# A decode block with its gradients on one core: the w1 gradient product of batch 0 taken from VectorE sums to TensorE pair transposes, and a second pass that starts two heads sooner

## The chip, the core and the metric

The kernel runs on one core of a Trainium2 chip. It is one launch. The metric is device time in microseconds (us), and less is better. The engines are called TensorE (PE in the profile), VectorE (DVE), ScalarE (ACT), GpSimd (POOL) and SyncE (SP). The profile is of one execution; the times are of several.

## What is computed

A pre-LayerNorm transformer block in decode (one query token, two batches), and all its gradients but those of a constant:

```python
B, D, H, Sk, Dh, Dff = 2, 640, 32, 4096, 128, 1728      # bf16 in and out
h  = x + softmax(q k^T * Dh**-0.5) v @ wo,   q = layernorm(x) @ wq     # per batch and head
h2 = h + relu(layernorm(h) @ w1) @ w2
out0 = h2
grads of (x, k_cache, v_cache, wq, wo, w1, w2) for a given grad_out    # jax.vjp
```

The two caches are 2 x 32 x 4096 x 128, that is 1 MiB for each batch, head and cache, and so are their gradients. All traffic together is 361.84 MB by the page.

## The kernel before, in words

**Two passes over the heads.** A head's tile is [128 positions, 32 chunks, 128 channels]. The first pass (`p1_iter`, one iteration `i` for each of the 64 pairs of batch and head) loads K and V of a head. It transposes K on TensorE by fp32 pairs (`pair_transpose`, L435: two bf16 columns are moved as one 32-bit word, and the copy at L440 brings the result from PSUM to SBUF), multiplies it with the query (`pair_matvec`, L448), exponentiates (L523), forms K weighted by the probabilities on VectorE (`pk`, L476), and sums on TensorE: `m_ps` (L469) and `u_ps` (L498). The second pass (`p2_iter` and `p2_tail`, one step `j` for each head) writes the gradients of K and V. For a step it needs V again (`W`), unless the tile was kept: the last six heads of a batch are kept, and they come first. It writes 2 MiB for each head (`gV` L900, `gK` L851, both from GpSimd's queue).

**The middle.** Between the passes over a batch lies `middle_gen(b)`: the sum over heads, the second LayerNorm, the MLP's hidden layer (`hf_ps`, L761), its gradient `ghfc`, then gx2 = w1 times `ghfc`, the backward LayerNorm (`gh1c`), and for each group of heads the gradient `go` with what the second pass needs (`go_group`). A head's second-pass step needs its `go_group`.

**The product gx2 = w1 times ghfc.** `spread_f` broadcasts the 14 columns of `ghfc` over the partitions (matmul L633, ScalarE copy L636) in three pieces, and 15 `ttr` instructions (L658, product and sum on VectorE) make the partial sums `gx2p`, which L794 adds up.

**The order is written out by hand.** There is a plan of iterations. `P2_AT = H + 2 + M0_ITERS` is the iteration at which the second pass joins, on every second iteration of the first. With M0_ITERS = 7 the middle of batch 0 has the iterations 34 to 40 for itself and the second pass joins at 41. From iteration 66 on there are second-pass steps alone (the tail), and batch 1's middle runs there. Background generators (the middles, `fin_gen` for the weight gradients, `gx_gen` for the gradient of x) are advanced a little after each of the eight parts of an iteration, by a credit: 0.8 for each part while a middle has the iterations for itself, 0.2 later; a bare `yield` costs 0.5. A `ttr` also waits for a `turn()`, of which an iteration in a middle gives five. If a head's `go_group` isn't issued when its step comes, `bg_until` issues all that is missing at once.

**Buffers.** 13 tiles of 1 MiB hold K, V, W and the gradients. `pump` issues loads in the order of the plan from SyncE's queue when the pool has a tile, and the load waits there for the last reader of the tile. From iteration 33 on six of the tiles are the kept V of batch 0.

Of the kernel before, what the change touches and what calls it, by code (L numbers as in the profile page):

```python
# [9 lines left out]
ALU = mybir.AluOpType  # L10
# [5 lines left out]
def kernel(  # L16
# [39 lines left out]
    NMT = (32, 12)  # L56
    NPS = 2 * H - 8

    def f_kc(c):
        return 128 if c < NFF else F_rem  # L60


# [11 lines left out]
    def pst(shape, dtype, role, name):  # L74

        k = banks[role].pop(0)
        banks[role].append(k)
        return ps.tile(shape, dtype, tag=f"bank{k}", bufs=1, name=name)
# [284 lines left out]
    NW2 = -(-NF // FP)  # L363
    w2_tiles = {}

    def load_w2(k, tag, order="(c p) d -> p c d"):

        c0, c1 = k * FP, min(NF, (k + 1) * FP)
        t = take(tag, [128, FP, D], "w2_t")
        full = min(c1, NFF)  # L370
        if full > c0:
            nc.sync.dma_start(out=t[:, 0:full - c0, :],
                              in_=B_w2[0:NFF * 128, :].rearrange(order, p=128)[:, c0:full, :])
        if c1 > NFF:
            nc.sync.dma_start(out=t[0:F_rem, NFF - c0, :], in_=B_w2[NFF * 128:Dff, :])
        return t
# [246 lines left out]
        nc.vector.tensor_tensor(out=Uc[:, b, :], in0=t[:], in1=rt[:, b, :], op=ALU.mult)  # L623


    def bcast_cols(colsrc, n, kc_of, dst, first=0):

        for c0 in range(0, n, 4):
            t = pst([128, 512], FP32, "bc", "bc_ps")
            w = 0  # L630
            for c in range(first + c0, first + min(n, c0 + 4)):
                kc = kc_of(c)
                nc.tensor.matmul(t[:, w:w + kc], lhsT=colsrc[0:kc, c:c + 1].to_broadcast([kc, 128]),  # L633
                                 rhs=ident_bf[0:kc, 0:kc], start=True, stop=True)
                w += kc
            nc.scalar.copy(out=dst[:, c0 * 128:c0 * 128 + w], in_=t[:, 0:w])  # L636
            yield

    def spread_cols(t, colsrc, n):
# [23 lines left out]
    def turn():  # L663

        while slot[0] <= 0:
            yield 0.0
        slot[0] -= 1

    def one(src, b):
        return src[:, :, b]  # L670
# [34 lines left out]
    def mlp_out():  # L705

        ml32 = fin.tile([128, ND, B], FP32, tag="ml32", bufs=1, name="ml32")
        nc.vector.memset(ml32[:], 0.0)
        while ("arow", 0) not in done:
            yield  # L710
        for k in range(NW2):
            while free["q"] < 1:
                yield
            t = load_w2(k, "q", "(p c) d -> p c d")
            yield from wait(12)
            c1 = min(NF, (k + 1) * FP)
            m_ps = pst([128, ND, B], FP32, "mid", "mlp_ps")
            for c in range(ND):
                for cf in range(k * FP, c1):
                    kc = f_kc(cf)  # L720
                    nc.tensor.matmul(m_ps[:, c, :], lhsT=t[0:kc, cf - k * FP, c * 128:(c + 1) * 128],
                                     rhs=arow[0:kc, cf, :], start=(cf == k * FP), stop=(cf == c1 - 1))
            give(t)
            yield
            nc.vector.tensor_tensor(out=ml32[:], in0=m_ps[:], in1=ml32[:], op=ALU.add)
        ml_bf = fin.tile([128, ND, B], BF16, tag="ml_bf", bufs=1, name="ml_bf")
        nc.vector.tensor_copy(out=ml_bf[:], in_=ml32[:])
        y_bf = fin.tile([128, B, ND], BF16, tag="y_bf", bufs=1, name="y_bf")
        nc.vector.tensor_tensor(out=y_bf[:].rearrange("p b c -> p c b"), in0=h1c[:], in1=ml_bf[:], op=ALU.add)
        yield from wait(3)  # L730
        for b in range(B):
            store_row(y_bf[:, b, :], ND, out_0[b].rearrange("s (c p) -> (s c) p", p=128))
            yield

    def middle_gen(b):
        if o_next[0] < (b + 1) * H // OG:
# [21 lines left out]
        for cf in range(NF):  # L758
            kc = f_kc(cf)
            for c in range(ND):  # L760
                nc.tensor.matmul(hf_ps[0:kc, cf:cf + 1], lhsT=w1_t[:, c, cf * 128:cf * 128 + kc],  # L761
                                 rhs=x2c[:, c, b:b + 1], start=(c == 0), stop=(c == ND - 1))
            yield 0.25
        nc.vector.tensor_scalar(out=acol[:, 0:NFF, b], in0=hf_ps[:, 0:NFF], scalar1=0.0, scalar2=None, op0=ALU.max)
        if F_rem:
            nc.vector.tensor_scalar(out=acol[0:F_rem, NFF, b:b + 1], in0=hf_ps[0:F_rem, NFF:NF],
                                    scalar1=0.0, scalar2=None, op0=ALU.max)
        mask = small.tile([128, NF], FP32, tag="mask", bufs=1, name="mask")
        nc.vector.tensor_single_scalar(out=mask[:], in_=acol[:, :, b], scalar=0.0, op=ALU.is_gt)
        nc.vector.tensor_tensor(out=ghfc[:, :, b], in0=ga[:, b, :], in1=mask[:], op=ALU.mult)  # L770
        yield from wait(3)
        gx2 = small.tile([128, 1, ND], FP32, tag="gx2", bufs=1, name="gx2")
        gx2p = small.tile([128, ND, 3], FP32, tag="gx2p", bufs=1, name="gx2p")

        def spread_f(k):
            r = rows3[:, 1 + k % 2, :]
            c0, c1 = k * ND, min(NF, (k + 1) * ND)
            yield from bcast_cols(one(ghfc, b), c1 - c0, f_kc, r, c0)
            rows.append((r, min(D, Dff - k * D)))

        rows = []
        yield from spread_f(0)
        for k in range(3):
            ahead = spread_f(k + 1) if k < 2 else iter(())
            r, fw_k = rows[k]
            for c in range(ND):
                yield from turn()
                ttr(w1_t[:, c, k * D:k * D + fw_k], r[:, 0:fw_k], gx2p[:, c, k:k + 1], fw_k)
                yield 0.85
                if c in (1, 3):  # L790
                    next(ahead, None)
            for _ in ahead:
                yield
        nc.vector.reduce_sum(out=gx2[:, 0, :], in_=gx2p[:], axis=AX.X)  # L794
        yield ("w1", b)
        yield from ln_bwd(gx2[:], x2c[:, :, b:b + 1], rstd2[:, b:b + 1], gc[:, :, b:b + 1], gh1c[:, :, b:b + 1], 1)
        hbc = rows3[:, 2, :]
        yield from bcast_cols(one(gh1c, b), ND, lambda c: 128, hbc)
        yield ("gh1", b)

        first = H - KEPT[b]
# [7 lines left out]
    def ga_gen():  # L809

        gbc = [rows3[:, 1 + b, :] for b in range(B)]
        for b in range(B):
            yield from bcast_cols(one(gc, b), ND, lambda c: 128, gbc[b])
        for k in range(NW2):
            while k not in w2_tiles:
                yield 0.0
            t = w2_tiles.pop(k)
            for c in range(k * FP, min(NF, (k + 1) * FP)):
                kc = f_kc(c)
                for b in range(B):  # L820
                    yield from turn()
                    ttr(t[0:kc, c - k * FP, :], gbc[b][0:kc, :], ga[0:kc, b, c:c + 1], D, kc)
                    yield 0.9
            give(t)
# [79 lines left out]

    fw = [0]

    def rows_of(pool, col, n, name, tag):

        r = pool.tile([128, n * 128], BF16, tag=tag, bufs=2 if tag == "rD" else 1, name=name)
        for c0 in range(0, n, 4):  # L910
            cn = min(4, n - c0)
            w = FIN["wide"][(c0 // 4) % 2]
            nc.scalar.copy(out=w[:, 0:cn, :, 0:B], in_=col[:, c0:c0 + cn, None, :].to_broadcast([128, cn, 4, B]))
            yield
            yield
            t = pst([128, 512], FP32, "mid", "rw_ps")
            for k in range(cn):
                nc.tensor.matmul(t[:, k * 128:(k + 1) * 128], lhsT=w[:, k, :, :].rearrange("p q x -> p (q x)"),
                                 rhs=ident_bf[:], start=True, stop=True)
            nc.scalar.copy(out=r[:, c0 * 128:(c0 + cn) * 128], in_=t[:, 0:cn * 128])  # L920
            yield 0.7
        FIN[name] = r

# [38 lines left out]
    def fin_gen(fin):  # L962
# [1 line left out]
        for w in FIN["wide"]:  # L964
            nc.vector.memset(w[:], 0.0)
        yield from wait(2)
        yield from rows_of(fin, acol, NF, "ar", "rX")
        ar_ps = pst([128, NFF, B], FP32, "mid", "ar_ps")
        for cf in range(NFF):
            nc.tensor.matmul(ar_ps[:, cf, :], lhsT=FIN["ar"][0:B, bass.ds(cf, 128, step=NFF)], rhs=ident_bf[0:B, 0:B],  # L970
                             start=True, stop=True)
        nc.scalar.copy(out=arow[:, 0:NFF, :], in_=ar_ps[:])
        if F_rem:
            nc.scalar.copy(out=arow[:, NFF, :], in_=acol[:, NFF, :])
        yield ("arow", 0)
        yield from rows_of(fin, gc, ND, "gr", "rD")
        yield from outer_rows(FIN["ar"], 0, NFF * 128, FIN["gr"], D, out_7[0:NFF * 128, :], NFF)
        if F_rem:
            yield from outer_rows(FIN["ar"], NFF * 128, F_rem, FIN["gr"], D, out_7[NFF * 128:Dff, :], 1)
        yield from rows_of(fin, ghfc, NF, "ghfr", "rX")  # L980
        yield from rows_of(fin, x2c, ND, "x2r", "rD")
        yield from outer_rows(FIN["x2r"], 0, D, FIN["ghfr"], Dff, out_6, ND)
        HH = H // 2
# [106 lines left out]
            assert bg and bg_one(bg) >= 0.0, mark  # L1090
        forced[0] = False

    M0_ITERS = 7
    P2_AT = H + 2 + M0_ITERS
    RATES = (0.2, 0.8, 0.2, 0.8, 0.45)
    RATE2 = 0.65
# [29 lines left out]
    def pump():  # L1126
        while queue:
            what, k = queue[0]
            if what == "w":
                load_weights(k)  # L1130
            else:
                tag = "ld"
                if free["ld"] < 1:
                    return
                if what == "w2":
                    w2_tiles[k] = load_w2(k, tag)
                else:
                    load_tile(what, k, tag)
            queue.pop(0)
# [142 lines left out]
```

## Time and profile before

| | |
|---|---|
| time, median of 3 runs | 897.04 us (895.9 to 898.17) |
| the profiled execution | 896.38 us, span 894.5 us |
| PE / DVE / ACT / POOL busy | 83% / 77% / 54% / 22% of the span |
| DMA over the span | 361.84 MB, 405 GB/s |
| chain that ended last | PE 40%, DMA 28%, DVE 17%, ACT 7%, issue 5% |

Busy time of PE counts the whole latency of pipelined matmuls: its pace is read from start to start. The chain's shares are averages over stages that have different limits, so the prediction reads the stage of batch 0's middle by itself.

### The profile page before, as it was taken

To read this page: it belongs to the slowest core of one execution; us is meant where nothing else is said; L and a number is where in the kernel's file an instruction comes from. 1 tells how busy PE (TensorE), PEld (TensorE's weight loads), DVE (VectorE), ACT (ScalarE), POOL (GpSimd) and SP (SyncE) were. 2 spreads that over 40 slices of the span, in tenths; PEclk is the share of its full clock that TensorE was granted. 3 is DMA by queue.
4 is the path that set the end of the run, shared out by engine and by line. 5 is a ranking of instruction groups with operands and counts; after the bars stand their busy time and mean duration, and the time that the engine had idled before them with its cause. 6 is when DMAs were issued, how large, how long until landed. Compare 5 with 4: busy or idle time off the path is not lost.

```text
span 894.5 us, 24705 instructions
## 1 busy us (share of the span) xinstructions
PE 744.0 (83%) x10145; PEld 619.9 (69%) x10145; DVE 684.9 (77%) x1283; ACT 483.4 (54%) x1236; POOL 196.1 (22%) x347
## 2 busy tenths in 40 slices
PE   4998899998998998798768786788798897988593
PEld 4887788888787887787657675567566665664453
DVE  2665788966888897697678896679886679978854
ACT  1443344443555665465446777776665765656462
POOL 1344434442210000000011231122221111111211
PEclk9999999999999999899895555555755756555555
DMA  9999999999989999999999999999999999999996
GB/s 376 419 411 404 409 407 419 410 414 410 364 299 374 421 423 424 424 420 424 406 374 399 416 418 421 385 417 389 421 421 411 422 425 425 425 425 426 423 407 271
DMA packets 56304, 361.84 MB, mean 405 GB/s; under 512 B 5696, under 2 KB 11904, under 8 KB 15488
## 3 DMA queue, kind: packets, MB, share of 16 engines
q1 hardware_dynamic: 34536, 211.13, 58.0%
q0 software_dynamic: 18432, 134.23, 36.1%
q10 hardware_dynamic: 3224, 14.92, 4.2%
q8 instruction: 80, 1.31, 0.6%
q14 instruction: 32, 0.26, 0.1%
HBM read 211.11 MB, written 149.13 MB: 403 GB/s over the span
## 4 chain that ended last, share of the span: by engine, by line
PE 40%; DMA 28%; DVE 17%; ACT 7%; issue 5%; SPq 0%; POOL 0%; ACTq 0%; POOLq 0%; DVEq 0%
PE t_ps L435 17%; DMA Vt<-in_A_v_cache_dram 12%; DMA out_dram<-gK 9%; PE m_ps L469 8%; DMA out_dram<-gV 5%; DVE gK L832 4%; DVE rows L658 4%; PE s_ps L448 3%; DVE gV L832 3%; DVE pk L476 3%; PE o_ps L950 3%; PE dp_ps L448 2%; ACT gV L899 2%; ACT t_sb L440 2%; PE u_ps L498 2%
## 5 line engine op out<-in xcount | busy, mean ns | idle before, releaser
L440 ACT COPY t_sb<-t_ps 128x512 f32<-128x512 f32 x479 | 271.9, 586 | 188.0 <-PE t_ps L435 184.5
L448 PEld LDWEIGHTS <-t_sb 128*128 128x128 bf16 x4096 | 169.8, 103 | 87.9 <-issue 39.8
L435 PE MATMUL t_ps<-ident_f,Wt 128*128 128x128 f32 x832 | 203.8, 398 | 0.7 <-ACT t_sb L440 0.7
L476 DVE TENSOR_TENSOR pk<-Kt,ep 128x2048 bf16<-128x2048 bf16 x128 | 156.2, 1221 | 42.5 <-ACT ep L523 23.4
L469 PE MATMUL m_ps<-pk,Vt 128*128 128x129 bf16 x2048 | 174.7, 223 | 16.7 <-DMA Vt<-in_A_v_cache_dram 15.4
L832 DVE TENSOR_TENSOR gK<-rb,gsp 128x2048 bf16<-128x2048 bf16 x128 | 153.0, 1223 | 15.1 <-DMA out_dram<-gV 13.3
L435 PEld LDWEIGHTS t_ps<-ident_f,Wt 128*128 128x128 f32 x832 | 142.4, 207 | 31.6 <-issue 23.6
L435 PE MATMUL t_ps<-ident_f,Kt 128*128 128x128 f32 x1024 | 149.7, 281 | 6.1 <-DMA Kt<-in_A_k_cache_dram 5.6
L832 DVE TENSOR_TENSOR gV<-rb,pp 128x2048 bf16<-128x2048 bf16 (+1 forms) x128 | 143.4, 1144 | 10.0 <-DMA out_dram<-gK 9.1
L469 PEld LDWEIGHTS <-Vt 128*128 128x128 bf16 x2048 | 129.9, 99 | 20.3 <-DMA Vt<-in_A_v_cache_dram 18.3
L435 PEld LDWEIGHTS t_ps<-ident_f,Kt 128*128 128x128 f32 x1024 | 113.3, 145 | 7.6 <-issue 4.9
L486 POOL COPY pk<-ep 128x16 bf16<-128x16 bf16 x80 | 83.0, 1039 | 151.6 <-ACT ep L523 111.9
L448 PE MATMUL dp_ps<-gom,t_sb 128*128 128x2 bf16 x2048 | 96.4, 168 | 19.0 <-ACT t_sb L440 18.5
L900 POOL DMA_DIRECT2D out_dram<-gV x64 | 34.2, 534 | 312.6 <-DVE nb L516 115.1
L448 PE MATMUL s_ps<-gom,t_sb 128*128 128x2 bf16 x2048 | 79.9, 164 | 1.5 <-DVE t_sb L438 1.5
L851 POOL DMA_DIRECT2D out_dram<-gK x64 | 34.0, 531 | 215.1 <-DVE gK L832 166.5
L582 ACT CAST MT<-m_ps 128x128 bf16<-128x128 f32 x64 | 17.0, 265 | 115.8 <-PE m_ps L469 115.8
L956 ACT CAST ot<-o_ps 128x512 bf16<-128x512 f32 (+3 forms) x152 | 67.6, 492 | 3.5 <-PE o_ps L950 1.9
L872 ACT ACTIVATE rb<-dp_ps,rt 128x256 bf16<-128x256 f32 x64 | 30.2, 471 | 42.4 <-PE dp_ps L867 41.2
L658 DVE CUSTOM_DVE_ANT_0 rows<-wo_t,rows 128x640 bf16<-128x640 bf16 x64 | 52.5, 820 | 0.2
L843 DVE SCALAR_TENSOR_TENSOR gsp<-dp_ps,negdot,P_bf 128x64 bf16<-128x64 f32 x64 | 17.9, 279 | 43.7 <-PE dp_ps L448 43.4
L658 DVE CUSTOM_DVE_ANT_0 rows<-wqs,gqr 128x1024 bf16<-128x1024 bf16 x40 | 48.8, 1219 | 0.2
(194 smaller groups left out, 759.5 us busy)
## 6 DMA issues: line engine op xcount, KB each, us to landing
Kt<-in_A_k_cache_dram SPq DMA_DIRECT2D x64, 1024.0 KB, 16.8
Vt<-in_A_v_cache_dram SPq DMA_DIRECT2D x64, 1024.0 KB, 17.0
out_dram<-gV POOLq DMA_DIRECT2D x64, 1024.0 KB, 12.2
out_dram<-gK POOLq DMA_DIRECT2D x64, 1024.0 KB, 12.9
Wt<-in_A_v_cache_dram SPq DMA_DIRECT2D x52, 1024.0 KB, 12.8
out_dram<-ot ACTq DMA_DIRECT2D x6, 960.0 KB, 8.6
wq_t<-in_A_wq_dram SPq DMA_DIRECT2D x5, 1024.0 KB, 7.0
wqs<-in_A_wq_dram SPq DMA_DIRECT2D x5, 1024.0 KB, 21.9
```

The source lines that it names most:

```text
L435: nc.tensor.transpose(t_ps[:, j, :], natf[:, 2 * cc:2 * cc + 2, :].rearrange("p c k -> p (c k)"), ident_f[:])
L440: nc.scalar.copy(out=t_sb[:], in_=t_ps[:])
L448: nc.tensor.matmul(dst[:, sc:sc + 2], lhsT=v[:, j, :, par], rhs=vecs[:, par, :], start=(par == 0), stop=(par == 1))
L469: nc.tensor.matmul(r["m"][:, 0:129], lhsT=r["V"][:, sc, :], rhs=r["pk"][sc // HALF][:, sc % HALF, 0:129], start=(sc == 0), stop=(sc == NSC ...
L476: nc.vector.tensor_tensor(out=p["pk"][k][:, :, 0:128].rearrange("p s (a two) -> p s a two", two=2), in0=p["K"][:, sl, :].rearrange("p s (a ...
L486: nc.gpsimd.tensor_copy(out=col, in_=e)
L658: nc.vector.tensor_tensor_reduce(out=junk[0:kc, 0:width], in0=in0, in1=in1, scale=1.0, scalar=0.0, op0=ALU.mult, op1=ALU.add, accum_out=acc)
L832: nc.vector.tensor_tensor(out=pairs_view(dst[:, sl, :]), in0=row.rearrange("p (a two) -> p a two", two=2)[:, None, :, :].to_broadcast([128 ...
L851: nc.gpsimd.dma_start(out=natural(out_2, bp, hp), in_=gK[:])
L872: nc.scalar.activation(out=rb[:], in_=bank[:, 128:384], func=ACT.Copy, scale=rt[:, b, h:h + 1])
L900: nc.gpsimd.dma_start(out=natural(out_3, b, h), in_=gV[:])
L956: nc.scalar.copy(out=ot[0:P, k, n0:n0 + nn], in_=o_ps[0:P, 0:nn])
```

## The change

In the middle of batch 0 gx2 is made by `w1_pairs`: w1, read as fp32 pairs, is transposed on TensorE in ten parts (four and three 128x128 blocks for each of the five chunks of D), ScalarE copies each part to SBUF (into `rows3`), and 70 matmuls with one column each add it up in PSUM. Batch 1 keeps the VectorE sums (`w1_sums`). So that the pairs line up, the hidden dimension is numbered by pairs everywhere: hidden column c holds every second f of a block of 256 (`f_of`, `f_kc`; twelve columns of 128, two of 96), `w1_t` is read with a stride of two by the hidden layer's matmuls and by ten of batch 1's sums, the first loads of w2 bring two neighbouring rows to a partition (`load_w2_pairs`), and `rows_of` turns `ar` and `ghfr` back to the plain order. M0_ITERS goes from 7 to 5.

```diff
+    NB2 = Dff // 256
+    KB2 = (Dff - NB2 * 256) // 2
     def f_kc(c):
+        return 128 if c < 2 * NB2 else KB2
+    def f_of(c):
+        return bass.ds(256 * (c // 2) + c % 2, f_kc(c), step=2)
...
+    def load_w2_pairs(k, tag):
...
+            nc.sync.dma_start(out=t[:, 0:full - c0, :].rearrange("p (k two) d -> p k two d", two=2),
+                              in_=B_w2[c0 * 128:full * 128, :].rearrange("(k p two) d -> p k two d", p=128, two=2))
...
+    def w1_pairs(b, dst):
+        tA = pst([128, 4, 128], FP32, "bc", "w1_psA")
+        tB = pst([128, 4, 128], FP32, "mid", "w1_psB")
+        nc.vector.memset(tB[96:128, 2, :], 0.0)
+        acc = tB[:, 3, 0:ND]
...
+        parts = [(c, t, x, k0, n) for c in range(ND) for t, x, k0, n in ((tA, xA, 0, 4), (tB, xB, 4, 3))]
+        for s in range(len(parts) + 2):
+            if s >= 2:
+                c, t, x, k0, n = parts[s - 2]
...
+                        nc.tensor.matmul(acc[:, c:c + 1], lhsT=v[:, :, par], rhs=ghfc[0:kc, cf, b:b + 1],
+                                         start=(cf == 0), stop=(cf == NF - 1))
+            if 1 <= s <= len(parts):
+                c, t, x, k0, n = parts[s - 1]
+                nc.scalar.copy(out=x, in_=t[:, 0:n, :])
+            if s < len(parts):
+                c, t, x, k0, n = parts[s]
+                for j in range(n):
+                    kc = f_kc(2 * (k0 + j))
+                    nc.tensor.transpose(t[0:kc, j, :], w1f[:, c, 128 * (k0 + j):128 * (k0 + j) + kc], ident_f[:])
+            yield 0.5
+        nc.vector.tensor_copy(out=dst, in_=acc)
...
-                nc.tensor.matmul(hf_ps[0:kc, cf:cf + 1], lhsT=w1_t[:, c, cf * 128:cf * 128 + kc],
+                nc.tensor.matmul(hf_ps[0:kc, cf:cf + 1], lhsT=w1_t[:, c, f_of(cf)],
...
+        if b == 0:
+            yield from w1_pairs(b, gx2[:, 0, :])
+        else:
+            yield from w1_sums(b, gx2[:, 0, :])
...
-    M0_ITERS = 7
+    M0_ITERS = 5
...
-                    w2_tiles[k] = load_w2(k, tag)
+                    w2_tiles[k] = load_w2_pairs(k, tag)
```

## The prediction

> **What bounds the kernel now.** I read the page first: its row by slices shows where the DMA engines are not full.
>
> ```profile
> DMA  9999999999989999999999999999999999999996
> GB/s 376 419 411 404 409 407 419 410 414 410 364 299 374 421 423 424 424 420 424 406 374 399 416 418 421 385 417 389 421 421 411 422 425 425 425 425 426 423 407 271
> ```
>
> Nearly everywhere it moves 400 to 425 GB/s: the kernel is bound by its 361.84 MB. The dip in slices 11 to 13 is batch 0's middle and the start of the second pass. An edit here gains what it takes from idle DMA time, and nothing else. Next the windows of that stage (columns: window, length, busy us and instructions by engine, TensorE clock, DMA share, GB/s).
>
> ```profile
> 226.90:258.50 31.60, 29.27 (x496) 25.52 (x497) 28.09 (x74) 16.38 (x47) 9.51 (x16) 1.00 0.89 351
> 258.50:285.00 26.50, 24.81 (x436) 22.26 (x437) 22.09 (x53) 16.06 (x44) 1.68 (x4) 1.00 0.85 316
> 285.00:336.00 51.00, 46.24 (x791) 40.74 (x789) 45.05 (x88) 31.28 (x87) 4.38 (x11) 1.00 1.01 423
> ```
>
> The first window is iterations 36 to 40, from one first `m_ps` matmul to that five iterations on; the second is the second pass getting under way. The later stage is full at 423 GB/s. An iteration loads 2.10 MB, 4.96 us at that pace, so the five need 24.8 us of their 31.6. Who holds them up? The chain of waits in 226 to 262:
>
> ```profile
> 229.33 0.82 DVE rows L658
> 230.20 0.83 DVE rows L658
> 231.13 1.11 DVE pk L476
> 232.34 0.73 DVE rows L658
> ...
> 237.66 1.14 DVE pk L476
> 238.90 0.73 DVE rows L658
> ...
> 255.30 0.55 PE u_ps L498 x8
> 256.41 0.49 PE m_ps L469 x8
> ```
>
> Until about 245 the chain goes mostly through VectorE: the sums to be removed (L658) and `pk`. Then mostly through TensorE. How much room has TensorE? Its timeline in iteration 37, whose paces are read from start to start:
>
> ```profile
> 232.77 0.63 PE L469 MATMUL m_ps<-pk,Vt 128*128 128x129 bf16 x8
> 233.29 0.60 PE L435 MATMUL t_ps<-ident_f,Kt 128*128 128x128 f32 x4
> 233.73 0.54 PE L448 MATMUL s_ps<-gom,t_sb 128*128 128x2 bf16 x16
> 234.14 0.39 PE L469 MATMUL m_ps<-pk,Vt 128*128 128x129 bf16 x4
> ...
> 237.44 1.04 PE L435 MATMUL t_ps<-ident_f,Kt 128*128 128x128 f32 x8
> 238.96 0.23 PE L514 MATMUL s_ps<-neg_ident,rmax 128*128 128x128 bf16 x1 [0.47 <-DVE rmax L568]
> ```
>
> Four fp32 transposes take 233.73-233.29 = 0.44 us, 0.11 each; 16 matvecs 0.41 us, 0.026 each. Added up so, an iteration is 5.2 us of TensorE: as much as its DMA. There is hardly a gap but the one before L514, which waits for VectorE. So TensorE has no room beside the first pass; what is put on it lengthens the stage.
>
> **The change, part by part.** *Removed from VectorE*: ten sums at 0.82 and five at 0.62 us, with their read-outs about 11.8 us, of which the stage gets back TensorE's gaps only. In 226.9 to 258.5 these gaps (before L514, L633 and between parts) and the 14 broadcasts (0.055 each, 0.8 us) are about 4 us. ScalarE loses five copies, 2.3 us.
>
> *Added to TensorE*: 35 fp32 transposes by 0.11 = 3.9 us, 70 one-column matmuls by 0.026 = 1.8 us: 5.7 us. *To ScalarE*: five copies of 512 columns at 0.588 (the group of `t_sb<-t_ps` in this window has 0.589) and five of 384 at about 0.48 (between 0.378 for 256 and 0.588 for 512): 5.3 us, on top of 3.4 us of the iteration's own copies, exponent and outputs. VectorE gets a memset and a copy, 0.3 us, hidden.
>
> *Where it lands.* I counted the yields. A part of an iteration gives 0.8 credit and a step of `w1_pairs` costs 0.5, so its twelve steps go into parts 2 to 7 of iteration 36; the backward LayerNorm follows in 37, the first two heads' `go_group` in part 5 of 38, ahead of step 0 at 39. So nothing is forced. The same count for the old kernel puts sums and groups where the trace has them.
>
> *Iteration 36, queue by queue*, from 227.36 (the third group's transposes). Three steps come in part 2, two each in parts 3, 4, 6 and 7, one in part 5. A part's matmuls need its copy, which stands on ScalarE behind the iteration's own. TensorE waits 0.47 us in part 2 (the copy ends at 229.2, behind the exponent and the copy of K's third group), 0.9 in part 3 (behind K's fourth group, to 232.1), 0.4 and 0.7 in part 7 (behind `MT` and `OU`). In order behind it stand the next iteration's transposes, and behind these all else. The sum is 5.2 + 5.7 + 2.4 = 13.3 us, where iteration 36 now takes 5.9. The load into a freed tile waits too: now SyncE issues it at 232.3; then `pk`'s second half must wait for `u_ps`, to about 235.5.
>
> *Iterations 37 and 38*: 5.2 and the LayerNorm's and broadcasts' 0.6 make 5.8; 5.9 for 38, as the last iteration (252.6 to 258.5) has, with the same two `go` sums. So 13.3 + 5.8 + 5.9 = 25.0 us for three, against 31.6 for five: **-6.6 us**.
>
> *The two iterations moved* become one more pair in the shared stage, with one step of the second pass, its K, V, W loads on SyncE and its two stores from GpSimd's queue. The stage is full of DMA. Six pairs from 336.5 to 443.2 take 17.8 us each: **+17.8**. The tail loses a step of 3.15 MB, at 425 GB/s **-7.4**. By DMA alone: three iterations need 14.9 us of 25.0, so 10.1 us idle instead of 6.8, +3.3, and the three terms above give +3.8.
>
> *w2*: packets of 1280 B took 59 ns and those of 8192 B 315 ns in 130 to 200 us; on the line between, 2560 B take 106. 1728 packets on 16 engines take 6.4 us, 864 longer ones 5.7: **-0.6** in a full stage.
>
> *Strides.* The hidden layer's weights with a stride of two: `pair_matvec` reads its weights so now, at 0.026, as L761 has without; 0. Batch 1's ten strided sums: 640 and 1024 columns take 0.820 and 1.219, 1.04 ns a column, and the copy of fp32 words (`t_sb`, 685 ns for 512) has the same slope with four bytes an element; I take 0, at most the double, 8.2 us of VectorE, in a stage where VectorE is 80 to 99% busy and DMA full. The pair copies in `rows_of` and the split one in batch 1 stay at ScalarE's column rate, at most 0.3 us and hidden.
>
> *The end.* The weight gradients' work keeps its tail step, so it ends one step nearer the end (their last store leaves at 873.3 of 894.5 now); `go` for batch 1 comes later by two steps `j`, still ahead of its use (heads 0 to 7 by 32, wanted at 33). -1 to +2 us; I take **+0.5**.
>
> Sum: -6.6 + 17.8 - 7.4 - 0.6 + 0.5 = +3.7. The profiled execution took 896.38, 1.9 above its span and 0.7 below the median, so 900.1 for it and 900.7 beside 897.04. A measurement here can tell 0.3%, 2.7 us, from no change: faster is below 894.3, slower above 899.7.
>
> **Does the burst keep its clock?** Here a rule of the Trainium skill meets the trace. At the start, after 18 us, TensorE has only K's transposes and matvecs, and the clock record goes to full at 21.6:
>
> ```profile
> 18.22 2.90 PE L435 MATMUL t_ps<-ident_f,Kt 128*128 128x128 f32 x12 [0.46 <-DMA Kt<-in_A_k_cache_dram]
> 20.92 0.61 PE L448 MATMUL s_ps<-gom,t_sb 128*128 128x2 bf16 x16
> 23.11 1.07 PE L435 MATMUL t_ps<-ident_f,Kt 128*128 128x128 f32 x8
> ```
>
> Twelve transposes take 2.70 us, 0.226 each; the eight at 23.11 are at 0.114. So transposes and matvecs alone brought the clock up and held it. The Trainium skill (TensorE: Matmul & The Clock Gate, Part 4: PE-mode transpose) says that transposes don't count as busy for the clock gate. By that rule the burst, with few other matmuls, would run at half clock; this trace speaks against it.
>
> **The rivals.** *B, the burst without waits* (same): copies keep ahead, iteration 36 takes 11.0: 898.4. For it: ScalarE is only 52% busy in the window; against: its queue is in order.
>
> *C, VectorE was the bound and the burst hides* (faster): the chain up to 245 speaks for it. If the loads under way cover the burst, idle time falls by two iterations' share, 2 x 1.7, and with w2 and the end: 897.0 - 3.4 - 0.1 = 893.5. It decides where iteration 36 takes no more than about 8 us; 10.9 us of TensorE work speaks against it, and that only seven tiles turn over in this stage.
>
> *D, half clock in the burst* (slower; the Trainium skill's rule above): the granted clock falls to half during a stretch of transposes. 43 of them, 0.116 more each, +5.0: 905.7. Against: the start; for: in the tail 0.5 is granted while TensorE does hardly more than transposes.
>
> *E, batch 1's strided sums cost double* (slower): 40% of 8.2 shows: 904.
>
> That the middle isn't done by 39 is excluded by the count, and the operations stand in the diff.
>
> **How the numbers follow.** The forecast 0.48 (own range 898.5 to 903), B 0.24, C 0.14, D 0.08, E 0.06. A sixth of the forecast's own case lies below 899.7: same 0.24 + 0.08 = 0.32, slower 0.40 + 0.14 = 0.54, faster 0.14. The range leaves out the lower part of C and the upper part of D: 894.5 to 905.5.
>
> **What would show it.** Iteration 36 of 12 to 14 us with TensorE waiting for ScalarE's copies of `w1_ps`, no `rows L658` in the chain there, a load gap of 3 us more; iterations 37 and 38 under 6 us; the joint stage at 420 GB/s again; transposes of `w1_ps` at 0.11. Wrong would be: iteration 36 under 9 us, a pace of 0.22, DMA under 400 GB/s after 285, or batch 1's sums over 0.9 us.

## The result, and the profile after

The changed kernel takes 903.78 us (median of six executions), the kernel before took 897.33 us in the runs beside it. One of the six took 961.47 us in a slower state of the chip and is left out of the comparison; the median of the other five is 902.89 us. The ratio of these is 1.0062, with an interval of 1.0044 to 1.0079: slower by 5.6 us, and by more than the 0.3% that a measurement can tell. The prediction was 900.7 us with a range of 894.5 to 905.5. The profiled execution took 902.89 us with a span of 900.9, against 896.38 and 894.5 before, so 6.4 us have to be found between the two traces. In the changed kernel the line numbers are later: K's transposes are L458, its copies L463, `m_ps` L492, `pk` L499, the VectorE sums L691, and the new product has its transposes in L796, its copies in L791 and its one-column matmuls in L787.

The page by slices, the row of throughput:

```profile
GB/s 378 418 415 409 410 390 419 410 414 404 255 284 397 423 422 424 421 422 424 422 396 400 407 421 420 399 365 396 416 412 417 421 420 424 425 426 421 424 407 288
```

The dip has the same place as before and is deeper: 255 and 284 GB/s in slices 11 and 12, where there were 364 and 299. In the first pass one more slice is clearly lower, the sixth (112 to 135 us) with 390 for 407; the experiments come back to it and call it slice 5, counted from 0. The windows of the stage (columns as before: window, length, busy us and instructions by engine, TensorE clock, DMA share, GB/s):

```profile
228.80:253.80 25.00, 22.74 (x378) 19.59 (x376) 12.43 (x36) 14.04 (x37) 5.48 (x10) 1.00 0.67 262
253.80:280.00 26.20, 24.57 (x431) 22.04 (x432) 21.29 (x49) 15.56 (x41) 1.47 (x3) 1.00 0.82 300
285.00:350.00 65.00, 57.72 (x984) 51.20 (x985) 54.00 (x106) 37.59 (x101) 6.00 (x14) 0.99 1.01 423
```

VectorE fell from 28.09 busy us of 31.6 to 12.43 of 25.0; it is no longer near a limit here. TensorE is still 91% busy, and the DMA moved 262 GB/s for 351. After 285 us the stage is full again, at the same 423 GB/s. The chain of waits in 226 to 258 (start, us, what):

```profile
229.38 0.51 PE w_psA L796 x4
229.91 0.59 ACT rows L791
230.91 0.50 PE w_psA L796 x4
...
240.36 0.49 ACT rows L791
241.20 0.93 PE t_ps L458 x8
```

There is no `rows` step of VectorE in it any more. In their place stand the product's transposes and ScalarE's copies, and K's own transposes, which queue behind them on TensorE. The timeline of TensorE in iteration 36 shows paces and waits (start, us, instruction; in brackets how long TensorE stood idle before it, and what ended that):

```profile
233.50 0.35 PE L787 MATMUL w_psB<-ghfc,rows 128*128 128x1 bf16 x8 [0.70 <-ACT rows L791]
...
236.25 0.34 PE L787 MATMUL w_psB<-ghfc,rows 128*128 128x1 bf16 x8
236.46 0.64 PE L796 MATMUL w_psA<-ident_f,w_t 128*128 128x128 f32 x4
236.93 0.63 PE L492 MATMUL m_ps<-pk,Vt 128*128 128x129 bf16 x8
...
240.89 0.30 PE L787 MATMUL w_psB<-ghfc,rows 128*128 128x1 bf16 x6 [0.63 <-ACT rows L791]
```

Read from start to start, eight one-column matmuls take 236.46-236.25 = 0.21 us and four transposes 0.47. And SyncE's queue shows what the long iteration does to the loads: the next K is issued 10.6 us after the last V, as its tile isn't free sooner.

```profile
226.65 0.33 SPq L479 DMA_DIRECT2D Vt<-in_A_v_cache_dram  x1
237.24 0.33 SPq L479 DMA_DIRECT2D Kt<-in_A_k_cache_dram  x1
```

To see where the 6.4 us lie, both traces can be cut at the exponents (`ep`) of the first pass, one for each iteration:

| piece | before | after | difference |
|---|---|---|---|
| start to `ep` of 36 | 226.89 | 228.85 | +2.0 |
| middle alone: 36 to 41 before, 36 to 39 after | 33.38 | 27.20 | -6.2 |
| shared stage, to `ep` of 63 | 182.95 | 198.65 | +15.7 |
| from there to the end of the span | 451.28 | 446.20 | -5.1 |

### The profile page after: what moved, and what is told of

It reads as the page before. It is cut to its first block, busy times and chain, and to the rows that moved or that the text cites. A ratio compares the mean times of both kernels' runs of the same rounds, so it can differ in the third digit from the quotient of the medians.

```text
span 900.9 us, 24850 instructions
## 1 busy us (share of the span) xinstructions
PE 747.5 (83%) x10237; PEld 624.8 (69%) x10237; DVE 676.0 (75%) x1256; ACT 486.0 (54%) x1238; POOL 194.9 (22%) x340
## 3 DMA queue, kind: packets, MB, share of 16 engines
q8 instruction: 80, 1.31, 0.6%
## 4 chain that ended last, share of the span: by engine, by line
PE 38%; DMA 31%; DVE 16%; ACT 8%; issue 5%; SPq 1%; POOL 0%; ACTq 0%; POOLq 0%; DVEq 0%
PE t_ps L458 16%; DMA Vt<-in_A_v_cache_dram 13%; PE m_ps L492 7%; DMA out_dram<-gK 7%; DMA out_dram<-gV 6%; DVE gK L905 4%; DVE rows L691 4%; DVE gV L905 4%; PE s_ps L471 3%; ACT gV L972 3%; ACT t_sb L463 3%; PE o_ps L1027 2%; DVE pk L499 2%; DMA wo_t<-in_A_wo_dram 2%; PE dp_ps L471 2%
## 5 line engine op out<-in xcount | busy, mean ns | idle before, releaser
L463 ACT COPY t_sb<-t_ps 128x512 f32<-128x512 f32 x479 | 272.4, 587 | 195.9 <-PE t_ps L458 191.1
L458 PE MATMUL t_ps<-ident_f,Wt 128*128 128x128 f32 x832 | 202.0, 394 | 0.7 <-ACT t_sb L463 0.7
L499 DVE TENSOR_TENSOR pk<-Kt,ep 128x2048 bf16<-128x2048 bf16 x128 | 156.3, 1222 | 53.1 <-ACT ep L546 30.1
L492 PE MATMUL m_ps<-pk,Vt 128*128 128x129 bf16 x2048 | 175.8, 224 | 16.4 <-DMA Vt<-in_A_v_cache_dram 15.7
L458 PEld LDWEIGHTS t_ps<-ident_f,Wt 128*128 128x128 f32 x832 | 140.6, 205 | 39.2 <-issue 32.0
L458 PE MATMUL t_ps<-ident_f,Kt 128*128 128x128 f32 x1024 | 151.3, 283 | 5.6 <-DMA Kt<-in_A_k_cache_dram 5.4
L492 PEld LDWEIGHTS <-Vt 128*128 128x128 bf16 x2048 | 131.0, 100 | 19.6 <-DMA Vt<-in_A_v_cache_dram 18.0
L458 PEld LDWEIGHTS t_ps<-ident_f,Kt 128*128 128x128 f32 x1024 | 114.7, 146 | 7.1 <-issue 4.3
L509 POOL COPY pk<-ep 128x16 bf16<-128x16 bf16 x76 | 81.0, 1068 | 150.7 <-ACT ep L546 105.2
L691 DVE CUSTOM_DVE_ANT_0 rows<-wo_t,rows 128x640 bf16<-128x640 bf16 x64 | 52.4, 819 | 0.4 <-ACT rows L668 0.2
L691 DVE CUSTOM_DVE_ANT_0 rows<-wqs,gqr 128x1024 bf16<-128x1024 bf16 x40 | 48.8, 1220 | 0.2
## 6 DMA issues: line engine op xcount, KB each, us to landing
out_dram<-gV POOLq DMA_DIRECT2D x64, 1024.0 KB, 11.5
Wt<-in_A_v_cache_dram SPq DMA_DIRECT2D x52, 1024.0 KB, 10.9
```

What stands on the lines that cost most here:

```text
L458: nc.tensor.transpose(t_ps[:, j, :], natf[:, 2 * cc:2 * cc + 2, :].rearrange("p c k -> p (c k)"), ident_f[:])
L463: nc.scalar.copy(out=t_sb[:], in_=t_ps[:])
L492: nc.tensor.matmul(r["m"][:, 0:129], lhsT=r["V"][:, sc, :], rhs=r["pk"][sc // HALF][:, sc % HALF, 0:129], start=(sc == 0), stop=(sc == NSC ...
L499: nc.vector.tensor_tensor(out=p["pk"][k][:, :, 0:128].rearrange("p s (a two) -> p s a two", two=2), in0=p["K"][:, sl, :].rearrange("p s (a ...
L509: nc.gpsimd.tensor_copy(out=col, in_=e)
L691: nc.vector.tensor_tensor_reduce(out=junk[0:kc, 0:width], in0=in0, in1=in1, scale=1.0, scalar=0.0, op0=ALU.mult, op1=ALU.add, accum_out=acc)
```

## The experiments

Each kernel was timed in five rounds against the kernel before on the same chip, so ratios are compared, not times. 0.001 of the ratio is 0.9 us. "Iteration" below is the time from one `ep` to the next.

**The numbering by pairs alone.** The changed kernel with VectorE sums in both batches and M0_ITERS = 7.

```diff
-        if b == 0:
-            yield from w1_pairs(b, gx2[:, 0, :])
-        else:
-            yield from w1_sums(b, gx2[:, 0, :])
+        yield from w1_sums(b, gx2[:, 0, :])
...
-    M0_ITERS = 5
+    M0_ITERS = 7
```

> The changed kernel with batch 0's product made by the VectorE sums again and the second pass joining at iteration 41 again. Only the numbering of the hidden dimension by pairs is left: the first loads of w2 in pairs of rows, w1 read with a stride of two. Theory: that part is worth -0.6 to 0 us against the kernel before (897). Rival: the 2 us that the changed kernel's profile is late by already when iteration 36 starts (226.9 against 228.9) are the numbering's, through the loads of w2 and w1 or their columns; then this kernel is 2 us slower than the one before, and its profile is late at 118 and at 222 us.

Measured: 899.15 us, ratio 1.0018 (1.0007 to 1.0030), +1.6 us. The rival was nearer: the numbering is not free. The windows of this kernel and then of the kernel before say where the DMA loses:

```profile
116.00:124.00 8.00, 7.77 (x135) 6.95 (x133) 6.79 (x14) 4.09 (x12) 4.04 (x4) 1.00 1.02 338
```

```profile
116.00:124.00 8.00, 8.00 (x150) 7.41 (x148) 7.09 (x15) 3.92 (x13) 2.72 (x3) 1.00 1.01 385
```

In these 8 us the third load of w2 is under way: 240 KB, now on 96 partitions, before on 128 and 64. The DMA engines are just as busy and move 47 GB/s less, 0.38 MB, 0.9 us of a full stage. Packets of 8192 B, those of K and V, took 353 ns on average in 112 to 126 us, for 329 before. In most profiles with this numbering part of it is paid 65 us later. Up to iteration 30 TensorE is the slower one and the loads run ahead; with less in reserve, TensorE meets a V that isn't there (timeline of TensorE, this kernel; the kernel before has no wait for a load between 120 and 200 us):

```profile
186.94 0.64 PE L492 MATMUL m_ps<-pk,Vt 128*128 128x129 bf16 x8 [1.19 <-DMA Vt<-in_A_v_cache_dram]
```

How much of that wait is loss can't be read from this profile alone. The granted clock falls to half for a while near 110 and 212 us in nearly every profile, and for how long varies: in 100 to 130 us it is 3.4 us before, 6.8 after, 0 in this kernel, which came to iteration 30 0.9 us ahead of the kernel before. A wait for V near 187 us, of 0.5 to 1.2 us, stands in nine of the eleven profiles with this numbering. It is missing in two, that of the changed kernel and one below (empty steps, 41), and these two had 6.8 us of half clock near 110: TensorE was late itself there. Seven profiles with the numbering had the same 3.4 us as the kernel before. Their `ep` of 31 comes at 192.81 to 193.24, before at 192.43, so 0.4 to 0.8 us of the cost may lie there. One profile of the kernel before isn't enough to say so: the kernel with thinner sums below, which doesn't have the numbering but 6.8 us of half clock, came at 193.56. Where the rest lies, single profiles don't show.

**Is it the length of w2's packets?** The same kernel, with one load for each of the two neighbours:

```diff
-            nc.sync.dma_start(out=t[:, 0:full - c0, :].rearrange("p (k two) d -> p k two d", two=2),
-                              in_=B_w2[c0 * 128:full * 128, :].rearrange("(k p two) d -> p k two d", p=128, two=2))
+            for par in range(2):
+                nc.sync.dma_start(out=...[:, :, par, :], in_=...[:, :, par, :])   # and so for the last 192 rows
```

> The pair numbering alone (as layout_only: VectorE sums in both batches, second pass at 41), with w2's first loads cut into one load for each of the two neighbours, so that a packet is again 1280 B and two loads take the place of each. layout_only was 1.0018 of the kernel before, 1.6 us. Theory: the third w2 load in packets of 2560 B on 96 partitions costs it: slice 5 moved 388 GB/s in every kernel with the pair numbering, 407 before, that is about 22 us x 19/407 = 1.0 us. Then this kernel is within 0.5 us of the one before, and slice 5 is back at 405 GB/s. Rival: the strides of two (the hidden layer's matmuls, the sums, the rows turned back) cost it elsewhere: ratio 1.0018 again. A third: the length of the packets doesn't matter but the 96 partitions do: slice 5 stays at 388 and the time at +1 to +2 us.

Measured: 898.12 us, 1.0017 (1.0003 to 1.0032), slice 5 at 388 GB/s, and again waits for V, the longest of 1.2 us. So the packets' length is not the cause; the 96 partitions remain as a candidate.

**Is it 96 partitions in one transfer?** The numbering alone, with the last 192 rows cut:

```diff
-            nc.sync.dma_start(out=t[0:KB2, full - c0:c1 - c0, :], in_=B_w2[full * 128:Dff, :].rearrange("(p two) d -> p two d", two=2))
+            for p0, p1 in ((0, 64), (64, KB2)):
+                nc.sync.dma_start(out=t[p0:p1, ...], in_=...[p0:p1])
```

> As layout_only (packets of 2560 B), with the third w2 load, 96 partitions in one transfer, cut into one of 64 and one of 32 partitions. Cutting all the loads to packets of 1280 B left slice 5 at 388 GB/s and the ratio at 1.0017. Theory: the spread of 96 partitions in one transfer slows what runs beside it; then slice 5 comes back to 400 to 407 GB/s and the time to within 0.8 us of the kernel before. Rival: any load of these rows beside K and V at this place does it, or slice 5 has nothing to do with the time: slice 5 at 388 and +1.5 us again.

Measured: 898.19 us, 1.0012 (0.9993 to 1.0030); slice 5 at 392, and 347 GB/s in 116 to 124 us. Between the two expectations, nearer to the rival, and the interval holds both no loss and the whole of it. Why this load slows its neighbours stays open; that it does, and that a wait for V follows at iteration 30, is in the traces.

**The product left out, and nothing in its place.** Batch 0's gx2 is set to zero; once with the second pass at 39, once at 41.

```diff
-            yield from w1_pairs(b, gx2[:, 0, :])
+            nc.vector.memset(gx2[:, 0, :], 0.0)
+            yield
```

> The changed kernel with no product of w1 and the MLP gradient in batch 0's middle at all: gx2 is set to zero there, so this part of the computation is left out. The second pass joins at 39. Theory: iterations 36, 37 and 38 take some 5.9, 5.8 and 7.0 us, 18.7 against 27.2 in the changed kernel: 8 us faster than that, 895 to 896 (1 to 2 us faster than before). This bounds what any cheaper product could bring. Rival (the earlier start is what costs): not under 899. Rival (the burst on TensorE is hidden behind loads): as the changed kernel, 903.

> No product in batch 0's middle (left out, gx2 is zero there), and the second pass joins at 41. Theory: an iteration that carries nothing takes 5.2 to 5.6 us of TensorE and needs 5.0 us of DMA, so two of them by themselves cost what two in the shared stage cost within 1 to 2 us: 894 to 897, the same as with the start at 39. Rival (two heads sooner is a gain of two slow iterations, 3 us): 3 us slower than with the start at 39.

Measured: 899.59 us, 1.0025 (1.0011 to 1.0039), and 904.71 us, 1.0087 (1.0072 to 1.0101). Both missed, the first by 3.6 us and the second by 7.7. That the first lies where the rival of the earlier start had it (not under 899) is chance, as the next experiment shows. The experiment changed more than it meant to: with the twelve steps gone, all that follows in the generator moves up at 0.8 credit a part, and the `go` sums of the next groups of heads, which belong to the shared stage, come in the middle. Thirteen sums of 640 columns stand on VectorE in 238 to 276 of the second kernel, TensorE waits for `goc` and `gom`, which VectorE makes behind them, and its clock falls (windows of the kernel with 41; the waits are shown in the last section):

```profile
246.00:252.00 6.00, 4.44 (x40) 4.23 (x40) 4.04 (x19) 1.81 (x6) 0.21 (x1) 0.60 0.81 298
252.00:258.00 6.00, 6.00 (x105) 5.33 (x104) 5.67 (x13) 2.01 (x6) 1.56 (x3) 0.83 0.47 162
```

**The product left out, its steps kept.** So that everything behind it keeps its place, twelve empty steps take the credit of the twelve real ones; for 41, sixteen empty parts (two iterations) more.

```diff
-            yield from w1_pairs(b, gx2[:, 0, :])
+            nc.vector.memset(gx2[:, 0, :], 0.0)
+            for _ in range(12):
+                yield 0.5
+            for _ in range(16):          # only with M0_ITERS = 7
+                yield 0.8
```

> The changed kernel, but the twelve steps of the product issue nothing (gx2 is zero there: the product is left out), so that everything behind them keeps its place in the order; the second pass joins at 39. In the two kernels without a product so far the sums for go moved up into the stage and filled VectorE there; here they can't. Theory: the burst on TensorE and its waits are worth what iteration 36 is longer by, 13.8 - 5.9 = 8 us: 895 to 897, DMA over 380 GB/s from 228 to 250. Rival: the stage is held by its seven tiles and the wait for loads, so that only a part of the burst shows: 899 to 901.

> As the kernel with twelve empty steps (product left out), but with sixteen more empty parts, so that the middle stands still for two iterations more and the second pass joins at 41. Alone against that kernel it is the price of two heads later with nothing else moved. Theory: two bare iterations take 11 us where two in the shared stage and a step fewer at the end took 9.6: 1 to 2 us slower than with the start at 39. Rival: a slow iteration costs 1.7 us more than its loads, 3.4 us slower or more.

Measured: 893.05 us, 0.9953 (0.9940 to 0.9966), and 894.35 us, 0.9967 (0.9955 to 0.9978). The first is 0.0109, 9.8 us, under the changed kernel (7 to 12.5 by the two intervals), and 2 us under the range that was expected; the second is 1.3 us slower than the first, as expected. A window of 19 us over nearly the same three iterations has a DMA share of 0.96 for 0.67, at 370 GB/s for 262 (in 228 to 250 us it is 373, where over 380 was expected):

```profile
226.90:245.90 19.00, 17.98 (x297) 15.84 (x298) 13.42 (x41) 9.93 (x28) 5.55 (x10) 1.00 0.96 370
```

Iterations 36 to 38 take 6.05, 5.86 and 7.45 us, together 19.36; in the changed kernel 13.84, 5.97 and 7.39, together 27.20. So the product on TensorE costs the stage 7.8 us, nearly all of it in iteration 36. Of the 10.1 us between the two spans 1.7 lie ahead of the stage and 0.7 in the shared stage. The two kernels also price the earlier start without the product: two heads sooner is worth 0.0014, 1.3 us, though the two intervals overlap. What the product cost on VectorE follows from two kernels with this numbering and the second pass at 41, the numbering alone (1.0018) and the empty steps (0.9967): 0.0051, 4.6 us (2.6 to 6.7 by the two intervals), and iterations 36 to 40 take 34.17 and 29.57 us in their profiles, 4.6 apart too. So the move to TensorE turned a cost of 4.6 us into one of 9.8 by the ratios, 7.8 of it seen in the stage. And the first kernel bounds the idea: a product that cost nothing would gain 4.2 us.

**The second pass at 41 again, with the pair product.** Only M0_ITERS goes back from 5 to 7.

> The changed kernel, its product on TensorE, but the second pass joins at iteration 41, as before the change. Theory: iteration 36 takes 13.8 us as in the changed kernel and 37 to 40 some 6.0, 5.5, 5.5 and 6.9, in all 37.7 against 33.4 us before, with the same work behind it: 4 to 5 us slower than before (901 to 902), and thus no better and no worse than the changed kernel by more than 3 us: the time is lost in iteration 36, not by the earlier start. Rival: the earlier start costs by itself, since a step more shares the first pass; then this kernel is at 897 to 898.

Measured: 907.3 us, 1.0123 (1.0102 to 1.0144), 5.5 us slower than the changed kernel: missed. The same cause as with the product left out: two more iterations at 0.8 credit bring the next groups' `go` sums into the middle, and iterations 36 to 40 take 14.83, 5.97, 6.52, 8.98 and 7.90 us, together 44.2 for the 37.7 expected. The earlier start is the part of the change that pays, and more than by its own 1.3 us, since it ends the fast rate when the first two heads' `go` is done.

**The waits for copies.** VectorE takes the five copies of 384 columns.

```diff
-                nc.scalar.copy(out=x, in_=t[:, 0:n, :])
+                if n == 3:
+                    nc.vector.tensor_copy(out=x, in_=t[:, 0:n, :])
+                else:
+                    nc.scalar.copy(out=x, in_=t[:, 0:n, :])
```

> The changed kernel with the five copies of three blocks (w1_psB) moved from ScalarE to VectorE, the five of four blocks left on ScalarE. Theory: TensorE's waits for copies in iteration 36 (0.5, 0.85, 0.4 and 0.7 us) mostly go, iteration 36 takes 11.5 to 12 us instead of 13.8: 1.5 to 2 us faster than the changed kernel, 902. Rival: the waits are for the order on TensorE or for DMA: no change.

Measured: 902.72 us, 1.0064 (1.0051 to 1.0078), no change. The time is near the 902 expected, but that is chance: iteration 36 takes 14.43 us, where 11.5 to 12 were expected. Its timeline of TensorE still has the waits:

```profile
233.05 0.35 PE L787 MATMUL w_psB<-ghfc,rows 128*128 128x1 bf16 x8 [0.70 <-ACT rows L794]
...
240.47 0.30 PE L787 MATMUL w_psB<-ghfc,rows 128*128 128x1 bf16 x6 [0.65 <-DVE rows L792]
```

The first (and one of 0.35 us before it) is for a copy of 512 columns, which stands on ScalarE behind K's own; the last is transpose, copy, matmul with nothing left to put between, whoever copies (VectorE's copy took 558 ns, ScalarE's 479).

**The same work, spread.** A step of `w1_pairs` costs 0.8 credit for 0.5, so one goes into a part.

> As the changed kernel, with a credit of 0.8 for each step of the TensorE product in place of 0.5, so that one step goes into a part and the twelve steps fill iterations 36 and 37 (parts 2 to 7 and 0 to 4) in place of one iteration; the first two heads' go is then issued all at once at step 0 of iteration 39. Theory: TensorE's own work of 5.7 us is what costs, wherever it lies, and the waits for copies are a smaller part: iterations 36 and 37 take together 17 to 19 us (19.8 in the changed kernel), the go at 39 costs 1 to 3 us of it again; 902 to 905 us. Rival: it is the one long iteration that costs (all behind it in TensorE's queue, the load gap of 10.6 us): the load gap falls below 7 us and the time to 899 to 901.

Measured: 902.92 us, 1.0065 (1.0045 to 1.0086): the same as the changed kernel, as the theory had it. Iterations 36 and 37 take 10.68 and 6.85, together 17.53 for 19.81, and 38 takes 9.55 for 7.39 with the late `go` group: 27.08 for 27.20. The gap in SyncE's queue is shorter by a quarter (V is issued at 226.51, K at 234.52, 8.0 us for 10.6), and nothing comes of it. So it isn't the one long iteration as such. The gap did not fall below the 7 us that the rival named, though, so a still flatter spread wasn't tried.

**VectorE's sums, thinner.** The other way to relieve VectorE: the kernel before, with three sums to an iteration in place of five until the product is done, and the second pass at 43.

```diff
-    M0_ITERS = 7
+    M0_ITERS = 9
-                slot[0] = {1: 2, 3: 1, 4: 1, 6: 1}.get(k, 0)
+                slot[0] = ({1: 2, 3: 1, 4: 1, 6: 1} if ("w1", 0) in done else {1: 1, 4: 1, 6: 1}).get(k, 0)
```

> The kernel before, but with three sums on VectorE in an iteration of batch 0's middle instead of five, so that they take two iterations more, and the second pass joins at 43. Theory: VectorE is then at 5.6 us in an iteration instead of 6.3, near the 5.2 of TensorE and the 5.0 of DMA; two iterations more by some 5.7 where the shared stage and the end gave 9.6: 36 to 42 take 41 us against 33.4, 1 to 2 us faster than the kernel before, 896. Rival: each iteration before the second pass costs some 2 us of idle DMA whatever VectorE does: 2 to 4 us slower, 900.

Measured: 898.99 us, 1.0020 (1.0005 to 1.0034), where 1 to 2 us faster was expected. In the stage iterations 37 to 41 take 5.2 to 5.9 us, near what was expected, but 36 and 42 take 7.21 and 7.45, and all seven 42.35 for 41. More was lost at the end of the first pass, where iterations 62 and 63 take 13.05 and 11.08 us (12.42 and 9.12 before), and behind the last store: it is issued at 880.24 for 885.12, but the span ends 16.0 us after it, 9.4 before. The window at the end of the first pass:

```profile
430.00:460.00 30.00, 24.26 (x355) 20.80 (x355) 19.90 (x40) 12.74 (x33) 4.16 (x8) 0.83 0.90 342
```

The kernel before moved 374 GB/s in the same 30 us. No version was found that computes the whole and beats the kernel before.

## Why the prediction was right, point by point

The time lies in the range and on the side that had the most chance, and the mechanism is the one forecast: the product costs more on TensorE than it cost on VectorE. That was shown by taking it out, on TensorE (7.8 us, in iteration 36) and on VectorE (4.6 us). The forecast had iteration 36 longer by 7.4 us (13.3 for 5.9), from 5.7 of work and 2.4 of waits.

*Iteration 36, 13.3 us forecast*: 13.84 from `ep` to `ep`, 13.89 by the prediction's own marks, the first `m_ps` matmuls. The four waits were 0.51, 0.87, 0.37 (in two pieces) and 0.76 us, read from start to start less one instruction's pace; forecast 0.47, 0.9, 0.4 and 0.7. Transposes came at 0.12 us for 0.11, which makes 35 of them 4.2 us for 3.9; the matvecs at 0.026. The copies were sized well (group of the changed kernel, middle alone; mean ns after the busy us):

```profile
L791 ACT COPY rows<-w_psA 128x512 f32<-128x512 f32 x5 | 2.9, 587 | 0.1
...
L791 ACT COPY rows<-w_psB 128x384 f32<-128x384 f32 x5 | 2.4, 479 | 3.9 <-PE w_psB L787 3.9
```

*Iterations 37 and 38, 5.8 and 5.9*: by the same marks 5.92 and 6.35, so the three took 26.16 us for 25.0 and the gain was 5.5 for 6.6. The term that was too small beside 36 is 38, which was read off the last iteration before. With the second pass about to join, VectorE has `pk` and eight small steps in a row, five of them of `go_group`, from 251.68 to 254.14, and TensorE waits for the last (timeline of the changed kernel):

```profile
254.19 0.23 PE L537 MATMUL s_ps<-neg_ident,rmax 128*128 128x128 bf16 x1 [0.66 <-DVE rmax L591]
```

*The two iterations moved, and the tail step, +17.8 and -7.4, with +0.5 for the end*: +15.7 and -5.1. One by one both are 2 us off, together they are +10.6 for +10.9: work that wasn't done by iteration 63 was done behind it. Here only their sum was forecast well.

*w2 and the strides, -0.6 and 0*: here is the error. The numbering by pairs alone cost 1.6 us (0.6 to 2.7), in its two variants 1.5 and 1.1 (0.3 to 2.9 and -0.6 to 2.7). The packets' length was counted, and right in itself (2560 B took 106 ns in the first two loads, the estimate), but not that throughput can fall while such a load is under way (the third one, whose own packets took 140 ns in the numbering alone), and that in most profiles TensorE would then wait for a V 65 us on. Of the strides, batch 1's sums cost nothing (E below) and the hidden layer's matmuls kept a median pace of 0.026 us. But the copies in `rows_of` that write every second element did not stay at ScalarE's column rate: `ghfr` and `ar` took 736 and 725 ns for 512 columns, 585 and 578 before, some 1.1 us of ScalarE in all. Whether that shows in the time no run separates.

Put together: the median is 5.6 us up where the sum gave 3.7. The numbering makes 1.6 for -0.6, that is 2.2; what is left, 4.0 for 4.3, held. In the profiles the cuts at the exponents give 2.0 - 6.2 + 15.7 - 5.1 = 6.4. Their first term is larger than the numbering's cost because of this execution: it had 6.8 us of half clock near 110 and again near 212 us where that of before had 3.4 each. Of the eleven profiles with the numbering the four with 6.8 us near 212, this one among them, are 1.6 to 2.0 us late at `ep` of 35, and the seven with 3.4 us 0.3 to 1.0.

*Rivals.* B (no waits) fell with the waits, and where two copies were moved or the work spread, the time stayed. C (VectorE was the bound and the burst hides) is half true: VectorE did hold the stage up, and with the second pass at 39 and the product gone from both engines the kernel is 4.2 us faster than before, near C's 893.5; but the burst doesn't hide. E (batch 1's strided sums) fell: the ten sums of 640 columns in batch 1's middle take 835 ns each in both profiles, with the stride and without. D (half clock in the burst) fell: the granted clock is 1.00 in 228.8 to 253.8, and transposes that ran at 0.12 us are not the 0.226 of the cold start. Why the clock is only 0.57 in the tail (700 to 800 us, kernel before) no run here separates. By the rule of the Trainium skill (TensorE: Matmul & The Clock Gate, Part 4: PE-mode transpose), that transposes don't count as busy, the clock should have fallen; this trace disagrees for fp32 transposes mixed with matvecs and the first pass's matmuls. The burst alone doesn't settle that rule, since about 5 us of its 13.8 were other matmuls (an estimate from the paces: 102 of one or two columns at 0.026, 32 of `m_ps` at 0.06, 8 of `u_ps` at 0.07). The start of the trace, in the prediction, is more direct: the clock went to full at 21.6 us after 2.70 us of transposes and 16 matvecs.

## What to carry to other kernels

An engine that is busy without being the bound can look like the place to take work from; first add up the engine that would receive it, in the one stage, from start to start: here it had almost no room, and 6.0 us of work (4.2 and 1.8) with 2.5 us of waits made the iteration 7.8 us longer. To price a piece of work in a schedule written as credits, leave empty steps in its place: cutting the steps as well moved other work into the gap, and a kernel with less to do became 8 us slower than before. A change of layout that goes with a change of engine should be measured by itself; here it was 1.6 us (0.6 to 2.7) of the 5.6.

## What the runs showed of the hardware that was not expected

*A load can slow the packets beside it at unchanged DMA share.* In 116 to 124 us, with the 96-partition load of w2 under way, the DMA share was 1.02 for 1.01 and the throughput 338 GB/s for 385. Packets of 8192 B took 353 ns for 329 (112 to 126 us), and where w2 came in packets of 1280 B these took 74 ns for 59. In all eleven profiles with this numbering slice 5 moved 388 to 392 GB/s, in the two without 407 and 408. Neither packets of half the length nor 64 and 32 partitions brought it back (334 and 347 GB/s in 116 to 124). The cause is open.

*The clock falls without a long gap.* With the product left out and the second pass at 41, TensorE waited 1.31 us and soon after 1.46 us (its timeline):

```profile
246.10 0.19 PE L356 MATMUL pr_ps<-goc,sel 128*128 128x4 bf16 x2 [1.31 <-DVE goc L714]
...
248.21 0.56 PE L721 MATMUL d_ps<-pr,ones_f32c 128*128 128x4 f32 x2 [1.46 <-DVE gom L361]
```

The clock fell in the second wait (windows of 1 us; TensorE busy us first, granted clock third from the end):

```profile
246.00:247.00 1.00, 0.65 (x14) 0.46 (x13) 0.96 (x3) 0.22 (x2) 0.00 (x0) 1.00 0.93 393
247.00:248.00 1.00, 0.00 (x0) 0.00 (x0) 0.95 (x7) 0.11 (x2) 0.00 (x0) 0.63 0.32 131
248.00:249.00 1.00, 0.79 (x8) 0.82 (x9) 0.34 (x3) 0.00 (x0) 0.00 (x0) 0.50 0.92 164
```

It falls at about 247.3 (0.63 is the mean of 0.26 us at 1.00 and 0.74 at 0.50) and is full again at 254.1. In the 3.4 us before the fall TensorE was busy for some 1.6 and idle for 1.8, the first 0.5 us of the second wait among them. In the kernel with the second pass at 39 it is the same a microsecond earlier. The Trainium skill (TensorE: Matmul & The Clock Gate, Part 1: The HAM clock gate) puts the fall behind an idle window of about 3.4 us. The low stretch, 6.8 us, is as long as two such windows, but no gap here was longer than 1.46 us, so here a window that was about half empty was enough. It isn't always: in the kernel before TensorE was busy for 1.62 us in 349.27 to 352.68, and the clock stayed at 1.00. What decides is open.
